# A spectral filter and a squared-ReLU FFN on one core: float32 inputs loaded by casting DMAs from the GpSimd queue, no casts on the engines

## The chip, the core and the metric

The kernel runs on one core of a Trainium2 chip. The metric is the device time of one execution in microseconds, lower is better. The engines are named as in the profile: PE (TensorE, matmuls; PEld is its weight load), DVE (VectorE), ACT (ScalarE), POOL (GpSimd) and SP (SyncE, which here only issues DMAs). A DMA can be issued from the queue of SP, ACT or POOL.

## The reference

The input x has 8 batches of 3008 positions and 256 channels. It is filtered along the positions in the frequency domain, and every position then goes through a two-layer FFN whose activation is a squared ReLU.

```python
x: (8, 3008, 256)   filt_r, filt_i: (1505, 256)
moe_w_in: (256, 2048)   moe_w_out: (2048, 256)        # all float32

X = np.fft.rfft(x, axis=1)
Y = X * (filt_r + 1j * filt_i)[None, :, :]
y = np.fft.irfft(Y, n=3008, axis=1).reshape(24064, 256)
h = np.maximum(y @ moe_w_in, 0.0)
out = (h * h) @ moe_w_out                             # (24064, 256) float32
```

## The kernel before

The transform length 3008 is split as 64 x 47, and forward and inverse transform are written as matmuls with constant float16 matrices (`sC0`, `sSB`, `sSP`). All matmuls take float16 operands and add up in float32 PSUM. The FFN runs over 47 groups (`g`) of 512 positions, in 8 slots (`s`) each.

**The steps for a batch b.**
- `unit_a` (or `chunk_a`, and `chunk_a0` for b = 0): first transform step from x in float16, evicted to `u`, written to the DRAM tile `dU[b]` by `write_u`.
- `read_u`, `unit_b`, `unit_s`, `unit_p`: `dU` is read back in another order (`ut`), the second step gives `psB`, DVE multiplies it with the filter `sF` (L453), and the first inverse step gives `ze`, written to `dZ[b]`.
- `read_z`, `unit_y`: `dZ` is read back (`zt`), and the last inverse step gives `yt`, the filtered batch, transposed, as the FFN takes it.

**The FFN.** `ffn_g1` multiplies `yt` with `sWin` into `psH`, and ACT applies the ReLU (L566) to `h2`. `ffn_sq` squares it on DVE (L570). `ffn_g2` multiplies with `sWout` into `psO` (L579), and `ffn_out` evicts that on ACT and writes it to DRAM. The first layer of group g and the second layer of group g - 1 alternate in the slots. The steps of the next batch are laid between them by `fft_plan`, a fixed plan of slots, so TensorE has FFN work beside each batch but the first.

**The prologue** is everything before the first second-layer matmul. It transforms batch 0 without going through `dU`: 26 matmuls on zeros (`warm`) start TensorE; `chunk_a0` works on x(0) (`xw16`, in three pieces of 1 MiB of float32); `turn_u` transposes; `place_f` spreads the two filter arrays over `sF` with selection matrices `sPF`, from `f16s[0]`, the filters in float16; `unit_b` and `unit_p0` do the second and third step. `sSPx` is a copy of `sSP` with its halves of partitions exchanged, made by 12 copies on POOL. Then `chunk_a` does the first step for batch 1 (chunks 0, 2, 1), and `unit_y` begins.

**How inputs get to float16.** The five float32 inputs are loaded by plain DMAs on SP's queue into float32 tiles, and engines cast them:
- x(0) and x(1): `load_wide` (L218), three pieces each, cast by `cast_wide` (L222) on DVE, POOL and ACT.
- The filters: `load_f` (L240) into tiles of 128 x 3008; the real one is cast on POOL (L674), the imaginary one in three parts on DVE, POOL and ACT (L222). The last filter row goes through `nyq`, two small DMAs of POOL's queue (L251).
- `moe_w_in`: `load_win` (L315) in seven pieces, cast on POOL by `cast_win` (L320).
- `moe_w_out`: `load_wout` (L328) in two halves, the first issued between the `read_z` of batch 0, cast on DVE by `cast_wout` (L333), four casts laid in slots 4 to 7 of the plan of batch 1.
- x(2) to x(7): `load_x` (L192) in four chunks a batch, cast on DVE by `cast_x` (L340) in the slots of the batch before.

The order of SP's queue in the prologue is written out by hand: x(0), real filter, `sPF`, imaginary filter, the second part of `sC0`, `sSB` and `sSP` in halves, `moe_w_in`, x(1), and then the writes of `dZ` and reads of `zt`. Each DMA signals its landing on one of eight semaphores in turn, so from the ninth on an issue waits for the landing of the one eight before it. The pools `p_x32` (2 buffers) and `p_x16` (4) hold x; `p_h2` (2 buffers, tag `h2`) holds in turn a piece of x(0), `uT`, `f16`, `ze_0`, the float32 `moe_w_out`, and then the activations of the groups.

Of the kernel before, what the change touches and what calls it, by code (L numbers as in the profile page):

```python
# [110 lines left out]
def kernel(  # L111
# [28 lines left out]
    p_x32 = ctx.enter_context(tc.tile_pool(name="p_x32", bufs=2))  # L140
    p_x16 = ctx.enter_context(tc.tile_pool(name="p_x16", bufs=4))
# [42 lines left out]
    x32s = {}  # L184

    def load_x(b, c, pool=None, tag="x32", q=None):

        t = (pool or p_x32).tile([96, 8, D], F32, tag=tag, name=f"x32_{b}_{c}")
        q = q or nc.sync
        if b + 1 < B:  # L190
            v = xrows[b * S:b * S + 96 * NM, :].rearrange("(p m) d -> p m d", m=NM)
            q.dma_start(out=t, in_=v[:, 8 * c:8 * c + 8, :])  # L192
        else:
            v = xrows[b * S:b * S + S, :].rearrange("(p m) d -> p m d", m=NM)
            q.dma_start(out=t[0:80], in_=v[0:80, 8 * c:8 * c + 8, :])
            q.dma_start(out=t[80:94], in_=v[80:94, 8 * c:8 * c + 8, :])
        x32s[(b, c)] = t
# [12 lines left out]
    xw32, xw16 = {}, {}  # L210

    def load_wide(b, k):

        v0 = xrows[b * S:b * S + 2048, :].rearrange("(p m) d -> p m d", m=16)
        v1 = xrows[b * S + 2048:b * S + 3072, :].rearrange("(p m) d -> p m d", m=8)
        pool, tag = (p_x32, "x32") if k < 2 else (p_y, "yt") if b else (p_h2, "h2")
        t = pool.tile([128, 8, D], F32, tag=tag, name=f"xw_{b}_{k}")
        nc.sync.dma_start(out=t, in_=(v0[:, 0:8, :], v1, v0[:, 8:16, :])[k])  # L218
        xw32[(b, k)] = t

    def cast(eng, out, in_):
        (eng.copy if eng is nc.scalar else eng.tensor_copy)(out=out, in_=in_)  # L222

    def cast_wide(b, k, *engs):
        t = p_x16.tile([128, 8, D], F16, tag="x16", name=f"xw16_{b}_{k}")
        for i in range(2):
            m = slice(4 * i, 4 * i + 4)
            cast(engs[i], t[:, m, :], xw32[(b, k)][:, m, :])
        xw16[(b, k)] = t

    for k in range(3):
        load_wide(0, k)


    f32s = []

    def load_f(im):
        filt = filt_i if im else filt_r
        t = p_y.tile([128, QF], F32, tag="yt", name=f"f32_{im}")
        nc.sync.dma_start(out=t, in_=filt[0:1504, :].rearrange("a d -> (a d)")  # L240
                          .rearrange("(p e) -> p e", e=QF))
        f32s.append(t)

    load_f(0)
    nc.sync.dma_start(out=sPF, in_=dPF.ap().rearrange("p (w q) -> p w q", q=128))
    load_f(1)
    nc.sync.dma_start(out=sC0[:, 704:1472], in_=dC0.ap()[:, 704:1472])
    nyq = p_out.tile([128, 2, D], F32, tag="ost", name="nyq")
    nc.gpsimd.memset(nyq, 0.0)
    for im, filt in enumerate((filt_r, filt_i)):  # L250
        nc.gpsimd.dma_start(out=nyq[0:1, im, :], in_=filt[1504:1505, :])  # L251
    sSB = const.tile([128, NC, 128], F16, name="sSB")
    sSP = const.tile([128, NC, 128], F16, name="sSP")
    sign = const.tile([128, 1], F32, name="sign")
# [15 lines left out]
    f16s = []  # L270

    def place_f(im, k, *engs, rotate=False):
# [6 lines left out]
        for i in range(4):  # L279
            c = 4 * k + i  # L280
            e0, e1 = D * c, D * (47 - c)
            cuts = [0] + [d for d in range(1, D)
                          if (e0 + d) % QF == 0 or (c and (e1 + d) % QF == 0)] + [D]
            for d0, d1 in zip(cuts, cuts[1:]):
                o = banks[i // 2][:, (i % 2) * D + d0:(i % 2) * D + d1]
                q, a = divmod(e0 + d0, QF)
                nc.tensor.matmul(o, sPF[:, PQ.index((0, q)), :], f16s[0][:, im, a:a + d1 - d0],  # L287
                                 start=True, stop=False)
                q, a = divmod(e1 + d0, QF) if c else (0, QF + d0)
                nc.tensor.matmul(o, sPF[:, PQ.index((1, q)), :], f16s[0][:, im, a:a + d1 - d0],  # L290
                                 start=False, stop=True)
# [12 lines left out]
    sWin = const.tile([128, 2, DFF], F16, name="sWin")  # L304
    sWout = const.tile([128, NJT, 256], F16, name="sWout")
    w32s = {}

    def load_win():

        for k, c, n, pool, tag in ((0, 0, 768, p_ze, "ze"), (0, 768, 768, p_ze, "ze"),  # L310
                                   (0, 1536, 512, p_prod, "prod"), (1, 0, 768, p_ze, "ze"),
                                   (1, 768, 512, p_prod, "prod"), (1, 1280, 512, p_prod, "prod"),
                                   (1, 1792, 256, p_yf, "yf")):
            t = pool.tile([128, n], F32, tag=tag, name=f"win32_{k}_{c}")
            nc.sync.dma_start(out=t, in_=moe_w_in[128 * k:128 * k + 128, c:c + n])  # L315
            wins.append((t, k, slice(c, c + n)))

    def cast_win():
        for t, k, c in wins:
            nc.gpsimd.tensor_copy(out=sWin[:, k, c], in_=t)  # L320

    wins = []

    def load_wout(k):
        if k == 0:
            w32s[2] = p_h2.tile([128, NJT, 256], F32, tag="h2", name="wout32")
        c = slice(8 * k, 8 * k + 8)
        nc.sync.dma_start(out=w32s[2][:, c, :],  # L328
                          in_=moe_w_out.rearrange("(jt r) c -> r jt c", r=128)[:, c, :])

    def cast_wout(k, eng):
        c = slice(4 * k, 4 * k + 4)
        eng.tensor_copy(out=sWout[:, c, :], in_=w32s[2][:, c, :])  # L333


    x16s, us, uts, prods, zes, zts, yts = {}, {}, {}, {}, {}, {}, {}

    def cast_x(b, c, eng=nc.vector):
        t = p_x16.tile([94, 8, D], F16, tag="x16", name=f"x16_{b}_{c}")
        eng.tensor_copy(out=t, in_=x32s.pop((b, c))[0:94])  # L340
        x16s[(b, c)] = t
# [6 lines left out]
    def unit_a(b, a):  # L348
# [6 lines left out]
        if b == 1:  # L355
            nc.tensor.matmul(ps[0:96, :], s1[:, c // 2, :], xw16[(b, 2 * (c % 2))][:, m, :],
                             start=True, stop=False)
            nc.tensor.matmul(ps[0:96, :], s1[0:120, 2 + c, :], xw16[(b, 1)][0:120, m, :],
                             start=False, stop=True)
        else:  # L360
            nc.tensor.matmul(ps[0:96, :], sSA, x16s[(b, c)][:, m, :], start=True, stop=True)  # L361
# [9 lines left out]
    def chunk_a(b, c):  # L371

        u = p_u.tile([96, 8, D], F16, tag="u", name=f"u_{b}_{c}")
        us[(b, c)] = u
        for k in range(2):
# [18 lines left out]
    def chunk_a0(c):  # L394

        for k in range(2):
# [213 lines left out]
    def fft_plan(b):  # L610
# [6 lines left out]
        if b == 1:  # L617
            for n in range(4, 16):
                put(n if n < 8 else n + 2 if n < 12 else 2 * n - 7, n % 2, unit_y, 0, n)
            for k in range(4):  # L620
                put((4, 5, 7, 7)[k], 1, cast_wout, k, nc.vector)
# [13 lines left out]
        if b + 1 < B:  # L635
            for c in range(2):
                put(t0 - 13, 1, load_x, b + 1, c)
            for c in range(4):
                r = t0 - 8 + 3 * c
                put(r, 1, cast_x, b + 1, c)  # L640
                if c < 2:
                    put(r, 1, load_x, b + 1, c + 2)
# [10 lines left out]
    for k in range(3):  # L653
        cast_wide(0, k, nc.vector, nc.gpsimd if k == 2 else nc.vector)

    def load_const(t, d, k):
        c = slice(12 * k, 12 * k + 12)
        nc.sync.dma_start(out=t, in_=d.ap().rearrange("p (a b) -> p a b", b=128)[:, c, :])

    for k in range(2):  # L660
        c = slice(12 * k, 12 * k + 12)
        load_const(sSB[:, c, :], dSB, k)
        load_const(sSP[:, c, :], dSP, k)
    load_win()
    for k in range(3):
        load_wide(1, k)
    for c in (0, 2, 1, 3):
        chunk_a0(c)
    f16s.append(p_h2.tile([128, 2, QF + D], F16, tag="h2", name="f16"))
    e0, e1 = slice(0, 1504), slice(1504, QF)  # L670
    for im in range(2):
        nc.gpsimd.tensor_copy(out=f16s[0][:, im, QF:], in_=nyq[:, im, :])
    for e in (e0, e1):
        nc.gpsimd.tensor_copy(out=f16s[0][:, 0, e], in_=f32s[0][:, e])  # L674
# [6 lines left out]
    for eng, e in ((nc.vector, slice(0, 1024)), (nc.gpsimd, slice(1024, 2048)),  # L681
                   (nc.scalar, slice(2048, QF))):
        cast(eng, f16s[0][:, 1, e], f32s[1][:, e])
# [10 lines left out]
    cast_win()  # L694
    for k in range(2):
        cast_wide(1, k, nc.gpsimd, nc.gpsimd)
# [10 lines left out]
    cast_wide(1, 2, nc.vector, nc.scalar)  # L707
    read_z(0, 0)
    load_wout(0)
    read_z(0, 1)  # L710
    load_wout(1)
    for c in (0, 2, 1):
        chunk_a(1, c)
    for c in (0, 2, 1):
        write_u(1, c)
    for n in range(4):
        unit_y(0, n)
# [52 lines left out]
```

## Time and profile before

| | us |
|---|---|
| median of 3 runs (793.4 to 793.72) | 793.63 |
| span of the profiled execution, first to last instruction | 791.9 |
| PE busy | 778.9 (98%) |
| ACT busy | 557.4 (70%) |
| DVE busy | 550.3 (69%) |
| POOL busy | 23.6 (3%) |
| `cast_x` on DVE (L340), 24 of 1.216 | 29.2 |
| `cast_wout` on DVE (L333), 4 of 0.68 | 2.7 |
| first `psO` matmul (L579) starts at | 60.84 |

The profile is of one execution whose span is 791.9 us. Its device time is given only with the runs, 793.4 to 793.72 us, so some 1.7 us lie outside of the span. A row of the timeline gives start, duration, engine, line, operation and `out<-in` by the program's names; in square brackets stands the idle time before it and what ended that. A queue is written SPq, ACTq or POOLq. A row of the windows gives, for a stretch of time, the busy time of each engine with its number of instructions, then the granted clock, the busy share of the 16 DMA engines and the GB/s moved. The chain of waits is followed back from the last instruction, and given in order of time.

### The profile page before, as it was taken

What the parts mean: (1) busy time and instruction counts of PE and PEld (TensorE: products, weight loads), DVE (VectorE), ACT (ScalarE), POOL (GpSimd) and SP (SyncE); (2) the same over time, 40 slices, a digit from 0 to 9 for tenths busy, and PEclk for the clock granted to TensorE, in tenths of its full rate; (3) what the DMA queues carried; (4) which work ended last, traced back from release to release, by engine and by line L of the source; (5) the groups of instructions that cost most, each with busy time, mean ns of one, the idle gap of its engine ahead of it and who ended that gap; (6) DMA issues with size and microseconds to landing.
All of it is one profiled execution on the core that took longest, in us unless ns stands there. A gap on an engine that the chain in (4) does not pass through costs nothing.

```text
span 791.9 us, 14822 instructions
## 1 busy us (share of the span) xinstructions
PE 778.9 (98%) x6102; PEld 552.5 (70%) x6102; DVE 550.3 (69%) x897; ACT 557.4 (70%) x711; POOL 23.6 (3%) x36
## 2 busy tenths in 40 slices
PE   8989999999999999999999999999999999999998
PEld 5746667667676777867777676776767677676666
DVE  6866994579755897559965699556995579553342
ACT  3976776777777777767776777676777777776664
POOL 3800000000000000000000000000000000000000
PEclk9999999999999999999999999999999999999999
DMA  9994554346814557154562555424563332611111
GB/s 363 368 260 153 146 157 111 93 135 167 205 42 112 167 155 180 48 173 135 132 167 65 163 147 155 112 80 148 159 180 86 97 133 66 147 40 41 41 41 54
DMA packets 88571, 107.32 MB, mean 136 GB/s; under 512 B 6336, under 2 KB 79040, under 8 KB 84288
## 3 DMA queue, kind: packets, MB, share of 16 engines
q1 hardware_dynamic: 88296, 106.19, 46.5%
q8 instruction: 48, 0.79, 0.4%
q10 hardware_dynamic: 144, 0.18, 0.1%
q14 instruction: 19, 0.16, 0.1%
q0 software_dynamic: 64, 0.00, 0.0%
HBM read 58.12 MB, written 48.23 MB: 134 GB/s over the span
## 4 chain that ended last, share of the span: by engine, by line
PE 89%; DVE 6%; DMA 3%; ACT 1%; SPq 0%; issue 0%; DVEq 0%; ACTq 0%
PE psO L579 40%; PE psH L562 38%; PE psA L361 3%; PE psY L532 2%; PE psB L445 2%; DMA f<-in_filt_i_dram 2%; PE psP L496 2%; DVE prod L453 2%; DVE h L570 1%; DMA wout<-in_moe_w_out_dram 1%; PE psf L287 1%; PE psf L290 1%; DVE yf L467 0%; ACT sF L298 0%; DVE yf L461 0%; ACT h L566 0%
## 5 line engine op out<-in xcount | busy, mean ns | idle before, releaser
L566 ACT ACTIVATE h<-psH 128x1024 f16<-128x1024 f32 x376 | 384.9, 1024 | 189.3 <-PE psH L562 186.7
L579 PE MATMUL psO<-sWout,h 128*128 128x256 f16 x3008 | 388.9, 272 | 0.6 <-DVE h L570 0.6
L562 PE MATMUL psH<-yt,sWin 128*128 128x512 f16 (+7 forms) x1728 | 386.9, 351 | 1.6 <-DVE yt L541 0.7
L579 PEld LDWEIGHTS <-h 128*128 128x128 f16 x3008 | 290.6, 98 | 79.1 <-DVE h L570 0.9
L570 DVE TENSOR_TENSOR h<-h 128x1024 f16<-128x1024 f16 x376 | 252.6, 685 | 104.7 <-ACT h L566 104.5
L562 PEld LDWEIGHTS <-sWin 128*128 128x128 f16 x1728 | 159.5, 98 | 101.7 <-issue 3.3
L453 DVE TENSOR_TENSOR prod<-psB,sF 128x1024 f16<-128x1024 f32 x84 | 102.3, 1218 | 2.8 <-PE psB L445 2.8
L541 DVE CAST yt<-psY 128x376 f16<-128x376 f32 x62 | 34.0, 549 | 59.4 <-PE psY L532 59.4
L367 DVE CAST u<-psA 96x512 f16<-96x512 f32 x50 | 34.3, 687 | 47.3 <-PE psA L361 45.1
L498 ACT CAST ze<-psP 128x512 f16<-128x512 f32 x84 | 49.1, 585 | 17.2 <-PE psP L496 14.7
L590 ACT COPY ost<-psO 128x512 f32<-128x512 f32 (+1 forms) x96 | 55.8, 581 | 6.8 <-PE psO L579 5.3
L532 PE MATMUL psY<-sC,zt 112*128 112x94 f16 x512 | 42.4, 205 | 1.4 <-DMA zt<-dZ 1.4
L532 PEld LDWEIGHTS <-zt 112*128 112x128 f16 x512 | 35.1, 98 | 11.6 <-issue 1.6
L467 DVE TENSOR_TENSOR yf<-prod,yf 128x512 f16<-128x512 f16 x84 | 35.7, 425 | 2.9
L361 PE MATMUL psA<-x,sC 94*96 94x512 f16 x96 | 36.6, 382 | 0.0
L445 PE MATMUL psB<-ut,sSB 128*128 128x256 f16 x192 | 36.5, 273 | 0.0
L496 PE MATMUL psP<-yf,sSP 128*128 128x256 f16 x168 | 32.1, 272 | 0.5 <-DVE prod L453 0.3
L539 ACT CAST yt<-psY 128x376 f16<-128x376 f32 x66 | 30.9, 468 | 2.0 <-issue 1.7
L445 PEld LDWEIGHTS <-sSB 128*128 128x128 f16 x192 | 18.5, 98 | 19.5
L340 DVE CAST x<-x 94x2048 f16<-94x2048 f32 x24 | 29.2, 1216 | 0.0
L365 ACT CAST u<-psA 96x512 f16<-96x512 f32 x50 | 28.6, 572 | 0.0
L460 DVE COPY yf<-prod 64x512 f16<-64x512 f16 x84 | 24.3, 289 | 2.9
(65 smaller groups left out, 253.2 us busy)
## 6 DMA issues: line engine op xcount, KB each, us to landing
x<-in_x_dram SPq DMA_DIRECT2D x20, 768.0 KB
zt<-dZ SPq DMA_DIRECT2D x64, 192.0 KB
dU<-u SPq DMA_DIRECT2D x28, 384.0 KB
dZ<-ze SPq DMA_DIRECT2D x28, 384.0 KB
out_dram<-ost SPq DMA_DIRECT2D x66, 128.0 KB
out_dram<-ost SPq DMA_DIRECT2D x31, 256.0 KB
ut<-dU SPq DMA_DIRECT2D x7, 1024.0 KB
xw<-in_x_dram SPq DMA_DIRECT2D x6, 1024.0 KB
```

The lines of the kernel that those rows point to most:

```text
L361: nc.tensor.matmul(ps[0:96, :], sSA, x16s[(b, c)][:, m, :], start=True, stop=True)
L445: nc.tensor.matmul(ps[:, i * D:(i + 1) * D], sSB[:, 2 * p + i, :], uts[b][:, 2 * p + i, :], start=True, stop=True)
L453: nc.vector.tensor_mul(out=prod, in0=ps.rearrange("p (a d) -> p a d", d=D).unsqueeze(1).to_broadcast([128, 2, 2, D]), in1=sF[:, :, 2 * p:2 ...
L467: nc.vector.tensor_add(out=yf, in0=prod[:, 0], in1=yf)
L496: nc.tensor.matmul(ps[:, i * D:(i + 1) * D], sSP[:, 2 * p + i, :], yf[:, i, :], start=True, stop=True)
L498: nc.scalar.copy(out=zes[(b, c)][:, 2 * i6:2 * i6 + 2, :], in_=ps.rearrange("p (a d) -> p a d", d=D))
L532: nc.tensor.matmul(ps[:, 94 * jj:94 * jj + 94], zt[:, 4 * (g % 2) + jj, dt * 128:(dt + 1) * 128], sSY, start=True, stop=True)
L562: nc.tensor.matmul(ps[:, i, o:o + n], sWin[:, dt, jt * 128:(jt + 1) * 128], yts[b][:, dt, r:r + n], start=(dt == 0), stop=(dt == 1))
L566: nc.scalar.activation(out=h2[:, 2 * s:2 * s + 2, :], in_=ps, func=AF.Relu)
L570: nc.vector.tensor_mul(out=v, in0=v, in1=v)
L579: nc.tensor.matmul(pso[g][:, t % 2, :], h2s[g][:, jt, t * 128:(t + 1) * 128], sWout[:, jt, :], start=(jt == 0), stop=(jt == NJT - 1))
L590: nc.scalar.copy(out=ost[:, h0:h0 + step, :], in_=pso[g][:, h0:h0 + step, :])
```

## The change

All float32 inputs are loaded by DMAs of POOL's queue whose destination is a float16 tile, so that the DMA casts. The float32 tiles, `p_x32` and all `cast_...` functions are gone; `p_x16` has 6 buffers. The constants `sPF`, `sSB`, `sSP` and the second part of `sC0`, which are float16 already, are loaded on POOL's queue as well, so that the order of the loads is that of one queue: x(0) in six DMAs of half a piece (all three first halves, then all three second halves), real filter, `sPF`, the last filter rows, imaginary filter, `sSB` and `sSP` in halves, `moe_w_in` in two DMAs, `sC0`, x(1) in three. `chunk_a0` is called with the half k as the outer loop. `moe_w_out` is loaded by one DMA, issued after a one-element copy on POOL (`first`) that reads the tile `u` of the last chunk of batch 1's first step. The later x loads stand four to a batch at one place of the plan, on POOL's queue.

```diff
-    p_x32 = ctx.enter_context(tc.tile_pool(name="p_x32", bufs=2))
-    p_x16 = ctx.enter_context(tc.tile_pool(name="p_x16", bufs=4))
+    p_x16 = ctx.enter_context(tc.tile_pool(name="p_x16", bufs=6))
...
+    def load_x(b, c):
+
+        t = p_x16.tile([96, 8, D], F16, tag="x16", name=f"x16_{b}_{c}")
+        n = 96 if b + 1 < B else 94
+        v = xrows[b * S:b * S + n * NM, :].rearrange("(p m) d -> p m d", m=NM)
+        nc.gpsimd.dma_start(out=t[0:n], in_=v[:, 8 * c:8 * c + 8, :])
+        x16s[(b, c)] = t
...
+    def load_wide(b, pieces):
 
         v0 = xrows[b * S:b * S + 2048, :].rearrange("(p m) d -> p m d", m=16)
         v1 = xrows[b * S + 2048:b * S + 3072, :].rearrange("(p m) d -> p m d", m=8)
...
+        v = (v0[:, 0:8, :], v1, v0[:, 8:16, :])
+        n = 8 // pieces
+        for i in range(pieces):
+            for k in range(3):
+                if i == 0:
+                    xw16[(b, k)] = p_x16.tile([128, 8, D], F16, tag="x16", name=f"xw16_{b}_{k}")
+                m = slice(n * i, n * i + n)
+                nc.gpsimd.dma_start(out=xw16[(b, k)][:, m, :], in_=v[k][:, m, :])
+
+    load_wide(0, 2)
+
+    f16 = p_h2.tile([128, 2, QF + D], F16, tag="h2", name="f16")
 
     def load_f(im):
         filt = filt_i if im else filt_r
...
+        nc.gpsimd.dma_start(out=f16[:, im, 0:QF], in_=filt[0:1504, :].rearrange("a d -> (a d)")
+                            .rearrange("(p e) -> p e", e=QF))
+
+    def load_const(t, d, k):
+        c = slice(12 * k, 12 * k + 12)
+        nc.gpsimd.dma_start(out=t[:, c, :], in_=d.ap().rearrange("p (a b) -> p a b", b=128)[:, c, :])
...
+    load_f(0)
+    nc.gpsimd.dma_start(out=sPF, in_=dPF.ap().rearrange("p (w q) -> p w q", q=128))
+    nc.vector.memset(f16[:, :, QF:], 0.0)
+    for im, filt in enumerate((filt_r, filt_i)):
+        nc.gpsimd.dma_start(out=f16[0:1, im, QF:], in_=filt[1504:1505, :])
+    load_f(1)
+    for k in range(2):
+        load_const(sSB, dSB, k)
+        load_const(sSP, dSP, k)
+    for k in range(2):
+        nc.gpsimd.dma_start(out=sWin[:, k, :], in_=moe_w_in[128 * k:128 * k + 128, :])
+    nc.gpsimd.dma_start(out=sC0[:, 704:1472], in_=dC0.ap()[:, 704:1472])
+    load_wide(1, 1)
...
+    def load_wout():
+
+        first = const.tile([1, 1], F16, name="first")
+        nc.gpsimd.tensor_copy(out=first, in_=us_last[0][0:1, 0, 0:1])
+        nc.gpsimd.dma_start(out=sWout, in_=moe_w_out.rearrange("(jt r) c -> r jt c", r=128))
...
-            for k in range(4):
-                put((4, 5, 7, 7)[k], 1, cast_wout, k, nc.vector)
...
-            for c in range(2):
+            for c in range(4):
                 put(t0 - 13, 1, load_x, b + 1, c)
-            for c in range(4):
-                r = t0 - 8 + 3 * c
-                put(r, 1, cast_x, b + 1, c)
-                if c < 2:
-                    put(r, 1, load_x, b + 1, c + 2)
...
-    for c in (0, 2, 1, 3):
-        chunk_a0(c)
...
+        for c in (0, 2, 1, 3):
+            chunk_a0(c, k)
...
-    cast_wide(1, 2, nc.vector, nc.scalar)
     read_z(0, 0)
-    load_wout(0)
     read_z(0, 1)
-    load_wout(1)
     for c in (0, 2, 1):
         chunk_a(1, c)
     for c in (0, 2, 1):
         write_u(1, c)
+    load_wout()
```

More of the change, by code (lines that the diff above doesn't have):

```diff
@@ L181, in pair_engine @@
         return nc.vector if npair[0] % 2 == 0 else nc.scalar
[L184 to L197, printed above, removed]
+    x16s = {}
+    def load_x(b, c):
[4 more added lines that the diff above has]
+        x16s[(b, c)] = t
     sC0 = const.tile([128, 1472], F16, name="sC0")
@@ L208 @@
     sPF = p_out.tile([128, 6, 128], F16, tag="ost", name="sPF")
-    xw32, xw16 = {}, {}
-    def load_wide(b, k):
+    xw16 = {}
+    def load_wide(b, pieces):
         v0 = xrows[b * S:b * S + 2048, :].rearrange("(p m) d -> p m d", m=16)
         v1 = xrows[b * S + 2048:b * S + 3072, :].rearrange("(p m) d -> p m d", m=8)
[L216 to L235, printed above, removed]
+        v = (v0[:, 0:8, :], v1, v0[:, 8:16, :])
+        n = 8 // pieces
@@ L237, in load_f @@
+        for i in range(pieces):
[6 more added lines that the diff above has]
+    f16 = p_h2.tile([128, 2, QF + D], F16, tag="h2", name="f16")
     def load_f(im):
         filt = filt_i if im else filt_r
-        t = p_y.tile([128, QF], F32, tag="yt", name=f"f32_{im}")
@@ L240, in load_f @@
[L240 to L251, printed above, removed]
+        nc.gpsimd.dma_start(out=f16[:, im, 0:QF], in_=filt[0:1504, :].rearrange("a d -> (a d)")
+                            .rearrange("(p e) -> p e", e=QF))
@@ L252 @@
+    def load_const(t, d, k):
+        c = slice(12 * k, 12 * k + 12)
+        nc.gpsimd.dma_start(out=t[:, c, :], in_=d.ap().rearrange("p (a b) -> p a b", b=128)[:, c, :])
     sSB = const.tile([128, NC, 128], F16, name="sSB")
     sSP = const.tile([128, NC, 128], F16, name="sSP")
+    sWin = const.tile([128, 2, DFF], F16, name="sWin")
+    sWout = const.tile([128, NJT, 256], F16, name="sWout")
+    load_f(0)
+    nc.gpsimd.dma_start(out=sPF, in_=dPF.ap().rearrange("p (w q) -> p w q", q=128))
+    nc.vector.memset(f16[:, :, QF:], 0.0)
@@ L268 @@
         nc.tensor.matmul(ps, zero, sF[:, 0, 0:2, :], start=True, stop=True)
-    f16s = []
     def place_f(im, k, *engs, rotate=False):
@@ L286, in place_f @@
                 q, a = divmod(e0 + d0, QF)
-                nc.tensor.matmul(o, sPF[:, PQ.index((0, q)), :], f16s[0][:, im, a:a + d1 - d0],
+                nc.tensor.matmul(o, sPF[:, PQ.index((0, q)), :], f16[:, im, a:a + d1 - d0],
                                  start=True, stop=False)
                 q, a = divmod(e1 + d0, QF) if c else (0, QF + d0)
-                nc.tensor.matmul(o, sPF[:, PQ.index((1, q)), :], f16s[0][:, im, a:a + d1 - d0],
+                nc.tensor.matmul(o, sPF[:, PQ.index((1, q)), :], f16[:, im, a:a + d1 - d0],
                                  start=False, stop=True)
@@ L302, in place_f @@
                 eng.tensor_copy(out=dst, in_=src)
[L304 to L341, printed above, removed]
+    def load_wout():
+        first = const.tile([1, 1], F16, name="first")
+        nc.gpsimd.tensor_copy(out=first, in_=us_last[0][0:1, 0, 0:1])
+        nc.gpsimd.dma_start(out=sWout, in_=moe_w_out.rearrange("(jt r) c -> r jt c", r=128))
+    us_last = []
+    us, uts, prods, zes, zts, yts = {}, {}, {}, {}, {}, {}
     def write_u(b, c):
@@ L360, in unit_a @@
         else:
-            nc.tensor.matmul(ps[0:96, :], sSA, x16s[(b, c)][:, m, :], start=True, stop=True)
+            nc.tensor.matmul(ps[0:96, :], sSA, x16s[(b, c)][0:94, m, :], start=True, stop=True)
         o = us[(b, c)][:, 2 * i:2 * i + 2, :]
@@ L374, in chunk_a @@
         us[(b, c)] = u
+        us_last[:] = [u]
         for k in range(2):
@@ L392, in chunk_a, with chunk_a0 @@
                     eng.tensor_copy(out=o, in_=pv)
-    def chunk_a0(c):
-        for k in range(2):
+    def chunk_a0(c, k):
+        if True:
             banks, groups = bank_pair(f"psA_0_{c}_{k}")
@@ L652 @@
     uT = p_h2.tile([128, 2, NC, 128], F16, tag="h2", name="uT")
[L653 to L658, printed above, removed]
-    for k in range(2):
[L661 to L666, printed above, removed]
-    for c in (0, 2, 1, 3):
-        chunk_a0(c)
[L669 to L674, printed above, removed]
+    for k in range(2):
+        for c in (0, 2, 1, 3):
+            chunk_a0(c, k)
     uts[0] = p_ut.tile([128, NC, D], F16, tag="ut", name="ut_0")
@@ L680 @@
     place_f(0, 0, nc.scalar, rotate=True)
-    for eng, e in ((nc.vector, slice(0, 1024)), (nc.gpsimd, slice(1024, 2048)),
-                   (nc.scalar, slice(2048, QF))):
-        cast(eng, f16s[0][:, 1, e], f32s[1][:, e])
     turn_u(4, nc.vector)
@@ L693 @@
         nc.gpsimd.tensor_copy(out=sSPx[-1][64:128, o, :], in_=sSP[0:64, c, :])
-    cast_win()
-    for k in range(2):
-        cast_wide(1, k, nc.gpsimd, nc.gpsimd)
     for k in range(7):
```

## The prediction

> **What bounds the kernel now.** I read the page's busy shares first, then the table of windows, the PE waits, the chain of waits by time, and the DMA view of single windows.
>
> ```profile
> PE 778.9 (98%) x6102; PEld 552.5 (70%) x6102; DVE 550.3 (69%) x897; ACT 557.4 (70%) x711; POOL 23.6 (3%) x36
> ...
> DMA  9994554346814557154562555424563332611111
> ```
> TensorE is busy for 98% of the span, and the DMA engines are full only in the first three of 40 slices (20 us each). So there are two stages with different limits. The windows show where the second begins (columns: PE, PEld, DVE, ACT, POOL busy, clock, DMA share, GB/s):
>
> ```profile
> 60.00:100.00 40.00, 39.51 (x300) 27.60 (x299) 32.94 (x58) 28.55 (x38) 0.00 (x0) 1.00 0.50 144
> 100.00:140.00 40.00, 39.23 (x345) 28.00 (x344) 29.11 (x48) 28.09 (x39) 0.00 (x0) 1.00 0.53 133
> 140.00:180.00 40.00, 40.00 (x280) 27.00 (x278) 27.33 (x45) 28.92 (x38) 0.00 (x0) 1.00 0.41 122
> ```
> From 140 us on PE has no idle time, so nothing taken off DVE there can pay. Between 60 and 140 us PE idles 0.49 + 0.77 = 1.26 us in all. What is left is the prologue, before the first `psO` (60.84 us in the PE timeline). Its chain of waits and its DMA view:
>
> ```profile
> 3.51 16.92 DMA f<-in_filt_i_dram
> 20.56 1.52 DVE f L222
> 22.13 0.28 PE psf L287
> ```
> ```profile
> DMA packets 1303, 7.07 MB, mean 416 GB/s; under 512 B 203, under 2 KB 530, under 8 KB 676
> ```
> The second fence is the window 3 to 20 us. The chain runs through the landing of the imaginary filter (20.43 us), its cast (1.52 us) and `place_f(1, 0)`; the loads before it move 416 GB/s with the DMA engines full. So **the prologue hangs on how fast the loads come**, and only second on the casts.
>
> **What the Trainium skill says.** "DMA: Bandwidth & Descriptors", section SWDGE vs HWDGE vs iDMA: a cast in a DMA can only be issued by GpSimd, where software on two of its cores writes the descriptors. The trace before has just two such DMAs, of 16 rows each and without a cast:
>
> ```profile
> 1.56 0.62 POOL L251 DMA_DIRECT2D nyq<-in_filt_r_dram  x1 [0.30 <-POOL nyq L249]
> 2.17 0.48 POOL L251 DMA_DIRECT2D nyq<-in_filt_i_dram  x1
> ```
> So an issue takes about half a microsecond; what 128 or 2048 rows take is not shown. The same page, section Issuing engines are not separate DMA queues: they all share the same 16 DMA engines. So the moved loads gain no bandwidth; the DMA row above, full on one queue alone, agrees. No section I found there gives a rate for a casting transfer. "SBUF — State Buffer", section SBUF: two separate sides: a VectorE operation in a two-port mode keeps GpSimd from writing descriptors. The two issues above lie beside the 0.91 us `zt` memsets of DVE and show no stall, so I price this at 0 to 1 us.
>
> **The change, part by part.** Times before are of the profiled execution, span 791.9 us; the runs have a median of 793.63, so 1.7 us lie around the span, and I add differences to 793.6.
>
> (1) Casts taken off. `cast_x` on DVE, 24 x 1.216 = 29.2 us; all of it after 101 us, where PE sets the pace. Two of them lie before 112 us, in the stretch with 0.77 us of PE idle: 0.4 us gained, 0 to 0.8. `cast_wout`, 4 x 0.68 = 2.7 us of DVE between 55.7 and 60.9, beside squares that PE waits for, and `yt` L541, for which PE waits 0.5 us at 59.76: 0.5 gained. `cast_wide` of x(0): hidden, since PE's 26 warm-up matmuls run to 10.4 us and `chunk_a0` then runs without a gap to 16.0. `cast_wide` of x(1) on DVE and ACT (0.68 and 1.05 us before the u copies): hidden, since the 24 matmuls of `chunk_a(1)` run on PE without a gap from 40.87 to 46.1. Cast of the filters: 22.13 - 20.43 = 1.7 us on the path, of which PE's own earlier work (`turn_u(5)`, to 21.4) covers 1.0. POOL's casts of `sWin` and x(1), 4.4 + 4.0 us: nobody waits.
>
> (2) Loads moved. 51 issues leave SP's queue, and POOL's grow from 2 to 46; SP's remaining writes and reads (dZ, zt, dU, out) come no earlier for it, since each waits for its data. Order and bytes stay nearly the same: x(0), f_r, sPF, f_i, sSB/sSP, win, sC0, x(1). From the ninth POOL issue on, each waits for the landing eight before it. Behind these waits stand the 12 `sSPx` copies; they follow the last x(1) issue, which waits for sSP's first half, and they need that half anyway: one issue, 0.6 us, under ACT's evictions (the first copies end at 24.2, `unit_p0(0)` is evicted at 27.7). In the steady part the x loads wait for PE's readers of `x16`; behind them stand only later x loads, some 20 us ahead of need. Priced at nothing; without PE's full queue as cover it would be a load of 3.1 MB, 7.5 us at 416 GB/s.
>
> (3) `sWout` in one DMA of 2048 rows of 1 KB, after `first`, a copy on POOL that waits for the third u chunk. Before, the halves are issued at 45.05 and 46.57 in SP's order, ahead of the dU writes. Now all of it comes after them or shares the engines with them, and `psO` waits for the whole of it.
>
> (4) x(0) in halves: nothing. The first halves would be there before PE leaves the warm-up.
>
> (5) **The rate of a casting transfer**, which no row shows. Bound from above by the plain 416 GB/s (reads and the half-sized writes overlap); from below I take half, 208. In between: if the write of half the bytes adds to the read, 1 / (1/416 + 0.5/416) = 277 GB/s. I take 277[...]; this is an estimate.
>
> Clock for it: DVE's casts show the x(0) pieces of 1.05 MB landing at 6.6, 9.1, 11.6, so the count starts at 4.1 us. At 277: x(0) 3.15 MB by 15.5, f_r 1.54 MB by 21.1, sPF 21.6, f_i by 27.2. `place_f(1, 0)` starts at 27.2 against 22.13: **+5.1**. Then ACT's loop of `sF` and `ze` (23.2 to 42.1) is as long as before, so `chunk_a(1)` could start at 40.9 + 5.1 = 46.0. The loads: sSB/sSP 1.57 MB plain 31.0, win 2.1 MB 38.6, sC0 39.1, x(1) by 46.7 (two pieces) and 50.5. Its third chunk starts at 50.5 (before 44.4), +6.1. `sWout` follows at about 53: 7.6 us alone, up to 14 with dU and zt in the way (the window 45 to 60 moved 291 GB/s), so 61 to 67; I take 66.5. First `psO` 66.5 against 60.84: +5.7. Less 0.4 of part (1), its other gains being inside waits that now end later: **+5.3, about 799 us**.
>
> **The rivals.**
> A, the forecast: casts run at 230 to 356 GB/s. 356 is the point of change: f_i's 6.23 MB then end at 22.1, as its cast did. 799.0, within 795 to 808.
> B, faster: the conversion costs no rate. Then f_i lands at about 20.5 as before, `place_f(1, 0)` starts at 21.4 when PE is free (0.7 gained); at 46.56 to 48.26 PE waits 1.4 us for zt, which no longer shares with sWout's first half (0.9 gained of it); 0.5 + 0.4 of part (1). Sum 2.5: 791.1. For it: the DMA engines write half the bytes into SBUF. Against: sWout must land by about 59.
> C: half rate, 208: f_i at 34.5, x(1) at 64.0, sWout at about 82: +21, 814.
> D: full rate, but `sWout` late, by its 2048 descriptors written in software and by sharing with dU and zt: `psO` at 62 to 65, +1 to +4, less 0.9 and the 0.7: about 795. Decides once sWout lands after 61.
> E: the change doesn't shorten anything because PE is full: B with its gains lost to the later start of POOL's queue, 793.6.
>
> **How the numbers follow.** A 0.38, B 0.27, C 0.13, D 0.14, E 0.08. 0.2% is 1.6 us, about what a measurement of this kernel can tell from no change. Faster by more: B with a little left out, 0.27; within: E and the near edge of D, 0.13; slower: A, C and most of D, 0.60. The range leaves out the faster end of B and the slow half of C: 790.5 to 814; A's own is 795 to 808. Predicted 799.0.
>
> **What would show it.** The DMA view of 3 to 20 us: about 277 GB/s read if A, 416 if B. In the chain `DMA f` should end near 27 us and be followed by `PE psf` without a cast. PE should wait longest for x(1) and sWout, and `psO` should start at 66 to 67. From 140 us the windows should be full as before. The prediction is wrong if f_i lands by 21 us, or if `psO` starts before 61, or if PE idles after 140 us on x loads.

## The result and the profile after

The changed kernel takes **820.25 us** in the median of 4 runs (818.42 to 824.02); the kernel before took 793.52 in runs beside it. The ratio is 1.0343, with an interval of 1.0317 to 1.0369: 3.4% slower. The profiled execution has a span of 817.5 us against 791.9, so 25.6 us have to be found in the trace.

First the page of the kernel after: busy shares, the PE clock by slices, and the groups of the second-layer and `psB` matmuls. Columns of a group: busy us, mean ns of one, then the idle time ahead of it and what ended it.

```profile
PE 789.1 (97%) x6102; PEld 556.4 (68%) x6102; DVE 520.4 (64%) x863; ACT 555.8 (68%) x709; POOL 32.4 (4%) x63
...
PEclk9998999999999999999999999999999999999999
DMA  9998224572246624284251942518125242431111
...
L543 PE MATMUL psO<-sWout,h 128*128 128x256 f16 x3008 | 392.8, 274 | 2.9 <-DMA sWout<-in_moe_w_out_dram 2.9
...
L409 PE MATMUL psB<-ut,sSB 128*128 128x256 f16 x192 | 37.3, 277 | 14.4 <-DMA ut<-dU 14.4
...
L190 POOL DMA_DIRECT2D x<-in_x_dram x24 | 12.2, 510 | 493.7 <-PE psA L324 473.9
```

DVE is relieved by 29.9 us (550.3 to 520.4), and of that PE gains 0.8 us. PE does the same 6102 matmuls but is *busy* 10.2 us longer, and it has two new waits: 14.4 us for `ut` ahead of `psB`, 2.9 us for `sWout` ahead of the first `psO`. Together that is 27.5 us; a few shorter waits elsewhere take some 2 us off. The last line is the cause in small: the x loads on POOL wait for nothing but PE's last read of an x buffer (`psA`).

The same three windows as before (60 to 180 us):

```profile
60.00:100.00 40.00, 33.48 (x222) 21.80 (x221) 22.21 (x38) 20.57 (x28) 1.01 (x2) 0.87 0.60 142
100.00:140.00 40.00, 39.54 (x314) 28.02 (x313) 28.91 (x52) 29.41 (x38) 0.00 (x0) 1.00 0.37 103
140.00:180.00 40.00, 36.86 (x288) 25.16 (x287) 20.40 (x32) 25.56 (x34) 2.02 (x4) 0.97 0.60 138
```

The window from 140 us on was full before. Now PE idles 3.1 us in it, POOL has four instructions in it (the x loads), and the clock is below 1. Following one and the same matmul of PE through both traces gives the lag of the kernel after: -0.9 us at the first `psY`, +2.1 at the first `psO`, +4.8 by 68 us, and +10.0 once the first `psB` of batch 1 and the slow stretch behind it are over. It falls to +9.3 at 123 us, where PE had waited 0.6 us for DVE in the kernel before (ahead of a `psO` at 114.16 us) and does so no longer. Behind batches 2 to 5 it is +14.0, +16.8, +21.2 and +25.7, and it stays there to the end. So the loss has one place in the prologue and five in the steady part, of 5.3, 4.7, 2.8, 4.4 and 4.5 us.

The **prologue**, in POOL's timeline and in the chain of waits of the kernel after (start, duration):

```profile
10.10 0.56 POOL L225 DMA_DIRECT2D f<-in_filt_i_dram  x1 [0.82 <-DMA xw<-in_x_dram]
...
22.05 0.53 POOL L217 DMA_DIRECT2D xw<-in_x_dram  x1 [1.64 <-DMA f<-in_filt_i_dram]
...
46.74 1.18 POOL L301 DMA_DIRECT2D sWout<-in_moe_w_out_dram  x1
47.91 2.03 POOL L190 DMA_DIRECT2D x<-in_x_dram  x4
```
```profile
19.80 2.01 ACT sF L291 x3
21.81 0.28 PE psf L280
...
46.74 16.11 DMA sWout<-in_moe_w_out_dram
62.90 1.87 PE psO L543 x8
...
70.47 7.19 DMA dU<-u
77.72 3.84 DMA ut<-dU
81.61 0.39 PE psB L409 x2
```

The chain names ACT's own eviction as what released `psf` at 21.81 (before 22.13), but the imaginary filter lands at the same moment, at 21.77 (11.67 us after its issue); the x(1) load that begins at 22.05 waited for that landing. In e1_gate, whose prologue has the same loads, `psf` waits 0.6 us for it. So the filter is still in the chain and only its cast is gone: it lands 1.3 us later than before (20.43), no cast of 1.5 us follows, and 0.3 us are gained. POOL spends 0.56 us on the issue of 128 rows and 1.18 us on that of 2048. But `sWout` needs 16.1 us from its issue to its landing, with x(2) issued right behind it.

The DMA view of 3 to 20 us answers the question of the rate:

```profile
DMA packets 1273, 3.37 MB, mean 198 GB/s; under 512 B 200, under 2 KB 200, under 8 KB 1272
```

It counts bytes where they are written, in float16. 3.07 MB of it are casts, for which twice as much is read, so some 380 GB/s are read over the window (an estimate), against 416 before. By single descriptors (one descriptor moves one contiguous piece), in the median: 8 KB of float32 written as 4 KB take 324 ns, a plain 8 KB 309 ns; for 1 KB to 512 B it is 60 against 46 ns.

**One batch of the steady part.** The chain of the kernel after (first fence) and SP's queue of the kernel before (second):

```profile
165.58 0.70 DVE u L330
166.33 7.89 DMA dU<-u
174.38 3.81 DMA ut<-dU
178.23 0.58 PE psB L409 x2
```
```profile
157.04 0.33 SPq L344 DMA_DIRECT2D dU<-u  x1
160.36 1.01 SPq L436 DMA_DIRECT2D ut<-dU  x2
```

From the last write of `dU` to the read of `ut`, which needs it landed, 3.3 us became 8.0. What lies between is in POOL's timeline of the kernel after:

```profile
161.49 0.51 POOL L190 DMA_DIRECT2D x<-in_x_dram  x1 [3.85 <-PE psA L324]
165.84 0.51 POOL L190 DMA_DIRECT2D x<-in_x_dram  x1 [3.85 <-PE psA L324]
```

PE's last `psA` of a chunk frees an x buffer, and DVE's eviction of that same `psA` releases the `dU` write. So **each x load starts about half a microsecond ahead of a `dU` write**: in the trace the load's descriptors run from 166.44 to 172.86 us, and the last one of `dU` ends at 173.9. In batches 1 to 5 of the kernel after this gap is 7.3, 8.0, 7.6, 7.7 and 7.7 us (before 3.3 to 3.7); in batches 6 and 7, where no x is left to load there, it is 3.3 again.

### The profile page after: what moved, and what is told of

It is laid out like the page before. It is cut to its first block, busy times and chain, and to the rows that moved or that the text cites. A ratio compares the mean times of both kernels' runs of the same rounds, so it can differ in the third digit from the quotient of the medians.

```text
span 817.5 us, 14752 instructions
## 1 busy us (share of the span) xinstructions
PE 789.1 (97%) x6102; PEld 556.4 (68%) x6102; DVE 520.4 (64%) x863; ACT 555.8 (68%) x709; POOL 32.4 (4%) x63
## 4 chain that ended last, share of the span: by engine, by line
PE 87%; DMA 9%; DVE 2%; ACT 1%; issue 0%; ACTq 0%; SPq 0%; POOL 0%; DVEq 0%
PE psO L543 38%; PE psH L526 36%; DMA dU<-u 5%; PE psB L409 3%; PE psA L324 3%; PE psY L496 2%; DMA ut<-dU 2%; PE psP L460 2%; DMA sWout<-in_moe_w_out_dram 2%; PE warm L263 1%; PE psf L280 1%; ACT sF L291 1%; PE psf L283 1%; DVE prod L417 0%; DVE u L330 0%; DVE prods L417 0%
## 5 line engine op out<-in xcount | busy, mean ns | idle before, releaser
L409 PE MATMUL psB<-ut,sSB 128*128 128x256 f16 x192 | 37.3, 277 | 14.4 <-DMA ut<-dU 14.4
L190 POOL DMA_DIRECT2D x<-in_x_dram x24 | 12.2, 510 | 493.7 <-PE psA L324 473.9
```

What stands on the lines that cost most here:

```text
L409: nc.tensor.matmul(ps[:, i * D:(i + 1) * D], sSB[:, 2 * p + i, :], uts[b][:, 2 * p + i, :], start=True, stop=True)
```

## Experiments

Theory **A**: the loads are free to start when a buffer is freed, which is just where the `dU` round trip is in a hurry; keep them away and the loss goes. Rival **B**: the casting, or the second queue, takes the DMA engines from SP's queue wherever the loads lie. Beside them stand the late `sWout` and a slow clock behind most of the waits. All kernels start from the one after, if nothing else is said.

**e1_gate.** A one-element copy on POOL holds the four x loads of a batch until a `ze` tile of their place in the plan is written.

```diff
     def load_x(b, c):
 
+        if c == 0:
+            gate = const.tile([1, 1], F16, name=f"gate_{b}")
+            nc.gpsimd.tensor_copy(out=gate, in_=ze_last[0])
         t = p_x16.tile([96, 8, D], F16, tag="x16", name=f"x16_{b}_{c}")
...
+        ze_last[:] = [zes[(b, c)][0:1, 2 * i6, 0:1]]
```


> The changed kernel, with one thing put back: the four x loads of a batch are held on POOL's queue until their place in the plan, by a one-element copy that reads the latest ze tile. Queue, cast, order and number of loads stay. Theory A (the loads are free to go as soon as an x16 buffer is read for the last time, which is when the last dU write is issued, and delay it): PE waits for ut vanish (14.4 us before), the gap from the last dU issue to the ut issue falls from 7.6 to about 3.3 us in every batch, and with the slow clock stretches after these waits some 21 of the 26.7 us go: 799 us, with what sWout costs (4 to 5 us) still there. Theory B (casting loads on the software queue are costly by themselves, whenever they run): at most 5 us go, 815 or more.

Measured: 796.68 us (793.63 to 798.98, 10 runs), ratio 1.003 (1.0018 to 1.0042); some 24 us of the loss are gone. What is left of PE's waits for DMAs, in its profiled run (793.63 us, the fastest of the ten):

```profile
PE psO L547 <- DMA sWout<-in_moe_w_out_dram: 1.8, 1, 1.8
...
PE psY L500 <- DMA zt<-dZ: 0.8, 1, 0.8
...
PE psf L283 <- DMA f<-in_filt_i_dram: 0.6, 1, 0.6
```

No wait for `ut`, and gaps of 3.1 to 3.2 us. The cast, the queue and the bytes are the same, only the time of the loads moved: A holds for the bulk. The other nine runs are 1.6 to 5.4 us longer, at a mean granted clock of 0.995 to 0.998. The one new wait that is left is that for `sWout`; e9_wout_plain tests whether it is the rest.

**e2_wout and e3_both.** `load_wout` without `first`, right behind the `sSPx` copies (about 32 us instead of 46.7), alone and with the gate of e1.

```diff
-        first = const.tile([1, 1], F16, name="first")
-        nc.gpsimd.tensor_copy(out=first, in_=us_last[0][0:1, 0, 0:1])
...
+    load_wout()        # behind the loop of sSPx copies
...
-    load_wout()        # behind the dU writes of batch 1
```


> The changed kernel, but sWout is loaded right after POOL's sSPx copies, without the copy called first. Theory A (the late sWout costs only in the prologue): PE's wait for sWout (2.9 us) and the half-clock stretch behind it go, 5 us: about 815 us, and the waits for ut in the later batches stay. Theory B (the wait for sWout sets the clock or the order of everything later): most of the 26.7 us go. If instead the DMA engines have no room between 33 and 45 us, zt comes late by the time sWout took, and nothing is gained.

> Both edits: x loads held until their place, sWout early. If the two costs add and nothing else is wrong with casting loads, the rest is the prologue's own gain (first psY 0.9 us earlier) and the freed DVE: 791 to 793 us, faster than before by 0 to 0.3%. If casting loads have a cost of their own, 795 or more.

Measured: e2 831.56 us, ratio 1.0463 (1.0429 to 1.0498); e3 798.94, ratio 1.0058 (1.0041 to 1.0075). Both are slower than expected, and e2 is some 11 us slower than the kernel after. PE's waits of e2, and its window of 50 to 60 us:

```profile
PE psB L407 <- DMA ut<-dU: 16.0, 5, 3.8
PE psY L494 <- DMA zt<-dZ: 13.9, 1, 13.9
```
```profile
50.00:60.00 10.00, 0.00 (x0) 0.00 (x0) 0.00 (x0) 0.00 (x0) 0.00 (x0) 0.50 0.75 175
```

No engine has an instruction for 10 us: the early `sWout`, and x(2), which POOL issues right behind it, delay the `zt` round trip, as the x loads delay that of `dU`. With the gate the `psY` wait is still 6.3 us. So `first`, which looks like a delay without purpose, keeps `sWout` off `zt`; an early load is no cure for a late one.

**e4_x_only.** The kernel before; only x(2) to x(7) go by casting loads on POOL, four to a batch at the place `t0 - 13` of the plan. `sWout` stays plain, on SP.

```diff
-        t = (pool or p_x32).tile([96, 8, D], F32, tag=tag, name=f"x32_{b}_{c}")
...
+        t = p_x16.tile([96, 8, D], F16, tag="x16", name=f"x16_{b}_{c}")
+        n = 96 if b + 1 < B else 94
...
+        nc.gpsimd.dma_start(out=t[0:n], in_=v[:, 8 * c:8 * c + 8, :])
...
-                put(r, 1, cast_x, b + 1, c)
```


> The kernel before, with only x(2) to x(7) loaded by casting DMAs on POOL's queue at the changed kernel's place in the plan (no float32 tile, no cast on DVE; p_x16 keeps 4 buffers). Prologue, filters and weights as before. Theory A (collision with the dU write): with 4 buffers each batch from 1 to 6 frees a buffer just ahead of its last dU write, so six waits for ut of about 2.5 to 3.5 us, four or more of them with a slow clock behind: 812 to 817 us. If the loss of the changed kernel came from the prologue, this one is at 793 or a little below.

Measured: 828.9 us, ratio 1.0436 (1.0403 to 1.0468), more than expected. PE's waits:

```profile
PE psB L433 <- DMA ut<-dU: 19.2, 6, 3.8
PE psY L520 <- DMA zt<-dZ: 4.3, 1, 4.3
```

This part alone loses 35 us, more than the whole change, so the bulk of the loss needs no casting load of x(0), x(1), filters or weights. Some 4 us of it are lost ahead of the first `psO`, where x(2) comes in among the reads of `zt`. Six batches wait here and five in the kernel after: with four buffers the last load of x(7) starts at 565.53 us, just ahead of the last `dU` write of batch 6 (566.02); with six buffers the last two went at 548.92 and 553.27, and the last write came at 562.47.

**e6_x_gate**: e4 with the gate of e1. **e10_x_gate_again**: the same kernel once more.

> The kernel before with only x(2) to x(7) by casting loads on POOL (as in e4_x_only), but held until their place in the plan by the one-element copy. Theory A (only the moment of the load matters): all of the 34 us go, 793 to 795 us, and the 29.2 us of DVE casts taken off bring nothing, since PE sets the pace. Theory B (the software queue or the cast slows the queue beside it whenever it runs): 800 or more.

> The kernel of e6_x_gate once more beside e9_wout_plain on the same chip: kernel before, x(2) to x(7) by casting loads of POOL's queue, issued at their place in the plan. It had 793.09 us and a ratio of 0.9988; if DVE's missing 29.2 us bring about 0.5 us between 101 and 112 us, it repeats at 0.998 to 0.9996; if that was chance, it comes out at 1.000.

Measured: 793.09 us, ratio 0.9988 (0.998 to 0.9996), and then 793.03, 0.9989 (0.9981 to 0.9997). All of the 35 us or so that e4 loses are gone with the gate. Taking 29.2 us of `cast_x` off DVE is worth 0.1%: in both traces PE's wait of 0.6 us for DVE ahead of the `psO` at 114 us is gone, and PE is 0.8 us further on from there.

**e5_warm.** 14 matmuls on zeros ahead of the first `psO` and of the first `psB` of batches 1 to 5, where PE would wait.

```diff
+    def fill(b=None):
+        ps = psF("fill")
+        for _ in range(14):
+            nc.tensor.matmul(ps, zero, sF[:, 0, 0:2, :], start=True, stop=True)
```


> The changed kernel with 14 matmuls of 512 columns on zeros (3.0 us at full clock) put ahead of the first psO and of the first psB of batches 1 to 5, where PE otherwise waits 2.6 to 3.4 us. Their result is read by nobody. Theory A (part of the loss is the slow clock that follows each long wait): the stretches at half clock (20.5 us in the profile, some 10 us of lost work) go, and the waits stay, filled: 809 to 812 us. Theory B (the waits alone are the loss): 820, or a little more by the fillers' overhang.

Measured: 813.13 us (811.48 to 813.54), ratio 1.0234 (1.0221 to 1.0247): some 7 us below the kernel after with more work on PE. The windows behind the wait for `sWout`, first of the kernel after, then of e5_warm (the last but two column is the clock):

```profile
60.00:65.00 5.00, 2.12 (x11) 1.44 (x10) 0.00 (x0) 1.17 (x2) 0.00 (x0) 0.66 1.15 213
65.00:70.00 5.00, 5.00 (x21) 2.55 (x20) 1.56 (x3) 1.49 (x2) 0.24 (x1) 0.65 0.66 133
```
```profile
60.00:65.00 5.00, 4.78 (x26) 2.50 (x26) 0.86 (x2) 1.77 (x3) 0.00 (x0) 1.00 1.17 215
65.00:70.00 5.00, 5.00 (x37) 3.26 (x35) 2.57 (x4) 2.19 (x3) 1.01 (x2) 1.00 0.84 149
```

From 65 to 70 us PE is fully busy in both, with 21 matmuls in the one and 37 in the other. The clock column is granted clock: the kernel after has five stretches at half of it, 6.83 us behind the `sWout` wait and four of 3.41 us at `psB` waits, 20.5 us in all, hence the 10.2 us of longer busy time. So some 7 us of the loss are slow clock behind the waits, not the waits themselves. The trace of the kernel after agrees: its batch 3, whose wait of 2.64 us has no slow stretch behind it, loses 2.8 us, and the other four lose 4.4 to 5.3. The gaps from `dU` to `ut` stayed at 7.3 to 8.3 us in e5_warm.

**e7_zt_first.** e1_gate with the last two `zt` reads and `sWout` issued ahead of the `dU` writes of batch 1.

```diff
     for c in (0, 2, 1):
         chunk_a(1, c)
+    load_wout()
+    for c in range(2, 4):
+        read_z(0, c)
     for c in (0, 2, 1):
         write_u(1, c)
-    load_wout()
...
-    for c in range(2, 4):
-        read_z(0, c)
```


> e1_gate with one more edit: in the prologue the reads of zt for chunks 2 and 3 are issued ahead of the three dU writes of batch 1, so fewer small packets stand ahead of sWout. If the dU writes are what holds sWout up, it lands 2 to 3 us sooner, PE's wait for it (1.8 us) goes, and the median falls by 1 to 3 us below e1_gate, to 793 to 795. If sWout's own 2048 rows set its landing, no difference: 796 to 797.

Measured: 796.51 us, ratio 1.0032 (1.002 to 1.0045), the same as e1; `psO` waits 2.4 us for `sWout`. This is the outcome expected for the case that the 2048 rows of `sWout` themselves set its landing. The trace shows a part of it: the first descriptor of `sWout` moves 4.8 us after its issue began, 4.3 us in e1_gate and 4.4 in the kernel after, though nothing stands ahead of it on POOL's queue; that of an x load of 96 rows moves within 1.2 to 1.9 us when that queue is empty.

**e8_sp_early.** The test of B: the kernel before, with its plain loads on SP's queue and its DVE casts; only the first two x loads of a batch are moved in the plan, to just ahead of the last `dU` write (in batch 1 they come 7.6 us ahead of it).

```diff
             for c in range(2):
-                put(t0 - 13, 1, load_x, b + 1, c)
+                put(9 if b == 1 else 13, 0, load_x, b + 1, c)
```


> The kernel before, all loads plain on SP's queue and all casts on DVE, with only the first two x loads of a batch moved in the plan to the slot of the last unit_a, ahead of the last dU write. No software queue, no cast in a DMA. Theory A (any bulk load ahead of the last dU write delays ut): 1.57 MB at 416 GB/s is 3.8 us, so the gap from dU issue to ut issue grows from 3.3 to between 5 and 7 us in batches 2 to 6, PE waits for ut 0 to 2.6 us each, 795 to 810 us. Theory B (it takes the second queue[...] or the cast): no change, 793 to 795.

Measured: 828.24 us, ratio 1.0418 (1.0397 to 1.0439). PE's waits and SP's queue in one batch:

```profile
PE psB L445 <- DMA ut<-dU: 21.4, 6, 4.7
```
```profile
157.11 0.92 SPq L192 DMA_DIRECT2D x<-in_x_dram  x2
158.94 0.69 SPq L344 DMA_DIRECT2D dU<-u  x1
167.83 0.82 SPq L436 DMA_DIRECT2D ut<-dU  x2
```

A gap of 8.9 us without a cast, without POOL and on one queue: neither is needed for the loss, and with e1 and e6, where both are present and the gap is short, B falls as the cause. The expectation of its size was too small. Two loads stand ahead of the write here and one in the kernel after, so whether a casting load on a second queue weighs more than a plain one is not shown.

**e9_wout_plain.** e1_gate, with `moe_w_out` alone loaded as before: float32, in two halves on SP between the `zt` reads, cast on DVE by four `cast_wout`.

```diff
     read_z(0, 0)
+    load_wout(0)       # plain float32 half, nc.sync
     read_z(0, 1)
+    load_wout(1)
...
+                put((4, 5, 7, 7)[k], 1, cast_wout, k, nc.vector)
```


> e1_gate with moe_w_out loaded as in the kernel before: plain float32 halves on SP's queue, issued between the first two read_z, and the four casts on DVE in slots 4 to 7. All other inputs stay casting loads. If the late sWout is what is left of the loss in e1_gate (its profiled run had psO at 61.66 us, with 1.8 us of waiting for sWout, and most of its runs a slow-clock stretch behind it), then psO starts at about 59.8 to 60.3 (before 60.84, less up to 1.1 us that psY was earlier in e1_gate), no slow-clock stretch follows, and the time is 792 to 793.2 us against 793.5 before. Rival: psY gains nothing, because zt now shares the engines with the float32 halves again and comes at 48.3 as before: 793.3 to 794. Rival two: with f16, uT, ze_0 and the float32 weights all in the two buffers of p_h2, the tile is free only late: psO after 61, 795 or more.

Measured: **791.69 us** (791.14 to 793.77, 8 runs) against 793.8 of before, ratio 0.9976 (0.9966 to 0.9986): the fastest of all, and a little below the 792 to 793.2 expected. Its chain of waits in the prologue:

```profile
44.02 3.15 DMA zt<-dZ
...
47.21 0.34 PE psY L507 x4
...
59.97 0.88 PE psO L554 x8
```

The first `psY` is 1.05 us earlier than before (47.21 for 48.26), and so is the first `psO` (59.8 for 60.84), without a wait for `sWout`. At 114 us another 0.8 is gained by the relief of DVE, and this stays to the end: 1.8 us. The profiled run of e1_gate ends where the kernel before does, 1.8 us behind e9, which is the length of its wait for `sWout`; and six of the eight runs of e9 have a mean granted clock of 1.000, where nine of the ten of e1 have 0.995 to 0.998. So the late `sWout` was what was left in e1: its wait in the profiled run, and in the others most likely a slow stretch behind that wait too, which no trace shows. Whether the earlier issue, the plain transfer or the other queue cures it was not separated.

## Why the prediction was wrong

The forecast was 799.0 us and slower; slower is right, for the wrong reason, and 820.25 lies beyond the range.

- **The step that failed is in (2): the steady x loads, "Priced at nothing".** I asked whether x comes in time for its reader and found 20 us to spare. I did not ask what else is on the DMA engines at the moment a load is set free. Before, a load stood in SP's queue behind what the plan put ahead of it; on POOL nothing stands ahead of it but the last read of its buffer, and that read comes just ahead of a `dU` write. PE's full queue did not cover the longer round trip: `psB` stands in PE's order where `ut` had been due, and all behind it waits. The measured price is 14.4 us of waits plus their slow clock; e1_gate gives back some 24 us, e6_x_gate all 35 of e4. The 7.5 us that I gave as the price without cover stand there once; a batch loses 2.8 to 5.3 us, and five of them do.
- **The slow clock was not in the sum at all.** e5_warm puts it at 7 us. "TensorE: Matmul & The Clock Gate", Part 1: The HAM clock gate (the "warmup" mystery), says that the array falls to half rate after an idle window of about 3.4 us and needs a busy window to come back. The trace agrees on half rate and on lengths (3.41 and 6.83 us), but shorter idle times are enough here: the clock fell at waits of 2.59 to 3.43 us, and at the one of 2.64 us in batch 3 it did not fall.
- **(5) was wrong**: 277 GB/s was taken, some 380 were read. The imaginary filter landed at 21.77 and `psf` started at 21.81, not at 27.2; of "wrong if f_i lands by 21 us" the trace came within a microsecond. Forecast A falls with it.
- **(3) was right in direction**: `sWout` came late and `psO` waited for it. `psO` started at 62.90, within the 62 to 65 of rival D and not at 66.5. Of the 16.1 us from issue to landing, 4.4 pass before the first descriptor of `sWout` moves; its 2048 descriptors of 63 ns in the mean are 8.1 us on 16 engines; the rest is sharing with `dU`, `zt` and x(2). That the first 4.4 us are the writing of the descriptors in software, as D has it, would fit e7_zt_first but is not shown, since SP's queue kept the engines full in that time. D's "about 795" is close to what the prologue alone does, 796.68 in e1_gate.
- **(4), and the issue costs in (2), were right**: x(0) in halves shows no gain in the chain, and the `sSPx` copies on POOL (24.5 to 32.4 us) held up nobody.
- **(1) was right**: the casts of `cast_x` were to give 0.4 us (0 to 0.8) by 112 us, and give 0.8 at 114 us. Rival B's 791.1 us is close to what e9_wout_plain does (791.69), once the loads keep their time and `sWout` its old place.

The check "PE idles after 140 us on x loads" was aimed at the right place but at the wrong wait: PE never waits for x, it waits for `ut`.

What stays open is why one load of 0.79 MB costs the round trip more than its own length. 96 descriptors of 324 ns on 16 engines are 1.9 us, yet the gap grows by 4.4. In the batch shown the load's descriptors took 458 ns in the mean and up to 1995, mixed with the 512-byte ones of `dU` and with output writes. "DMA: Bandwidth & Descriptors", section Queues, rings and completion order, says that an engine switches between queues only at the end of a packet of several descriptors; that would fit a `dU` write that ends only after the load, but e8_sp_early has such a gap on one queue, and no run here tells packets apart.

## What to carry to other kernels

When a load moves to another queue, ask what had held it back, and what will be on the DMA engines when its buffer is freed; a load with 20 us to spare still costs if it starts just ahead of a short write-and-read-back that the busiest engine waits for. A one-element copy that reads a tile of the right moment is enough to hold it. Count a wait of some 3 us on TensorE at more than its length, for the half clock that follows most of them.

## What the runs showed of the hardware

- A casting DMA from float32 to float16 reads at nearly the plain rate: 324 against 309 ns for 8 KB. Its issue occupied POOL for 0.51 to 0.69 us with 96 or 128 rows and for 1.18 us with 2048. From the start of the issue to the first descriptor it was 1.2 to 1.9 us for 96 rows and 4.3 to 5.1 us for 2048, each with nothing ahead of it on POOL's queue (kernel after, e1_gate, e5_warm, e6_x_gate, e7_zt_first).
- In the kernel after the granted clock fell to half five times, for 3.41 us or twice that, at 61.63, 82.11, 177.68, 375.66 and 474.64 us. These are 6, 28, 58 and 29 times 3.413 us apart, so the falls lie on a fixed grid of that length. In the grid step ahead of each fall PE was busy for 0.50 to 1.36 of 3.41 us. The wait of batch 3 (2.64 us) lies across two steps, with PE busy for 1.47 and 2.71 us, and the clock did not fall. The busy time of one step is not the whole rule: the clock fell after 1.85 us in e5_warm (at 48.98 us) and did not after 1.42 us in e4_x_only (at 576.77 us).
- A load of 0.79 MB beside a `dU` write stretched the gap to the read-back from 3.3 us to between 7.3 and 8.0; two plain ones on the same queue ahead of it made it 8.2 to 9.4 in five of six batches.
